# A drain on GpSimd, the count of flagged batches and the branch behind it, and a new order of loads

## The chip, the cores and the metric

The kernel runs on one core of a Trainium2 chip: TensorE (PE in the rows, with PEld for its weight loads), VectorE (DVE), ScalarE (ACT), GpSimd (POOL) and SyncE (SP), and 16 transfer engines that all queues share. A name with a q (POOLq) is an engine's sequencer, which takes instructions in order and hands them on. The metric is the time of one execution on the device in microseconds (us). In the rows the granted clock is a share of TensorE's 2.4 GHz.

## The reference

Attention with pooled keys and values, then a router that sends each row to one of eight experts. B = 8 batches, H = 8 heads, S = 576 rows, D = 64; the rows of a batch are 512 wide (all heads side by side).

```python
k_p = k.reshape(B, H, 72, 8, D).mean(axis=3)
v_p = v.reshape(B, H, 72, 8, D).mean(axis=3)
attn = softmax(q @ k_p.T / 8)
x = (attn @ v_p).transpose(0, 2, 1, 3).reshape(4608, 512)
logits = normalized(x) @ normalized(expert_emb).T / tau
expert_idx = argmax(logits)
gate_w = softmax(logits)[expert_idx]
for e in range(8):
    out[mask] = gate_w * (relu(x[mask] @ w1[e]) @ w2[e])    # 512 -> 1024 -> 512
```

## The kernel before

**One batch, one expert.** The kernel guesses one expert for each batch from the mean of its pooled values, loads the weights of that expert alone, and runs all 576 rows of the batch through it. It then looks whether a row chose another expert than the guess, or lies outside a number range. Such a batch is flagged, and a second pass behind the main part (`attend_again` and the loops around it) does it again, with every expert that is present. With these inputs no batch is flagged.

**Steps of a batch b.** Each step has a name. POOL loads K, Q and V rows, converting to 16 bits (K*b*, Q*b*.0, V*b*; for batch 0 in two parts each). DVE adds up groups of eight rows of V (VA, VB) and of K (KA, KB; in batch 0 TensorE does KA). TensorE takes the mean of the values (GM) and multiplies it with the experts' embeddings (GL); DVE finds the best (GD); PK reads that number into POOL's registers, and W1*b* and W2*b* are loads of the expert's two weight matrices, 1 MB each in 16 bits, whose addresses come from it. TensorE transposes the keys (KT, copied by KE), makes scores (SC), ACT the exponentials (EX), TensorE the weighted values (PV), DVE divides (XM), TensorE transposes (XT, copied by XE into xt). RT and RE find each row's best expert, NA to ND the gate. The FFN is H (16 steps, each 4 matmuls, relu by HE) and Y (four chunks of 128 rows, 8 matmuls each, and YL for the last 64 rows), scaled by YE, YF and YG and stored by SP (ST, SL; the second half of the very last chunk by ACT).

**The order.** `Plan.order` makes one fixed order for all engines before anything runs, in a model of times: at each point it takes the step that can start soonest, among equals the one with the lowest priority number, to which TUNED adds a value by name. The loads are an exception: they are issued in the order of LOADS. Where the model sees TensorE wait, `keep_warm` matmuls without use are put ahead of the step (L813). The weights have four buffers, K, V and Q two each, the output tiles 18. A store waits for one load of the list BEHIND. Everything inside `tc.manual_schedule()` is issued in this order; what is written behind that block is placed by the framework, which may issue an instruction sooner where nothing holds it.

**Behind the main part** stand a drain of POOL (L996), a read of the number n_i into the registers of all five engines (L997), and the second pass, a loop from 0 to that number. n_i is made by `presence`: PR, PP (a matmul, L869) and PX (eight short DVE steps, L872 to L884), whose priority puts them at the very end.

Lines of the rows: L319 loads K or V rows, L325 Q rows, L343 W1, L349 W2, L359 is PK's read, L448 the additions of VA and KA, L518 GL, L523 and L524 GD, L548 transposes q, L650 copies xt, L707 H, L719 Y, L725 YL, L733 YF, L337 stores.

Of the kernel before, what the change touches and what calls it, by code (L numbers as in the profile page):

```python
# [16 lines left out]
ALU = mybir.AluOpType  # L17
# [46 lines left out]
}  # L64
LOADS = """
V0.0 V0.1 K0.0 K0.1 Q0.0 Q0.1 V1 PK0 W10 K1 Q1.0 W20 V2 PK1 W11 K2 Q2.0 V3 W21 V4 K3 PK2 W12
Q3.0 PK3 W22 K4 W13 Q4.0 V5 Q5.0 PK4 W23 W14 K5 K6 V6 PK5 W24 W15 Q6.0 V7 Q7.0 PK6 W25 K7
W16 PK7 W26 W17 W27
# [145 lines left out]
def kernel(  # L214
# [103 lines left out]
    def load_rows(a, b, raw, g0=0, g1=G):  # L318
        return nc.gpsimd.dma_start(  # L319
            out=raw.rearrange("p h t d -> p h (t d)")[g0:g1],  # L320
            in_=a[b].rearrange("h (g t) d -> g h (t d)", g=G)[g0:g1])
# [86 lines left out]
    def attention(b, base, xt):  # L408
# [8 lines left out]
        for c, src, raw in (("V", v, vr), ("K", k, kr)):  # L417
            if b == 0:
                add(n(c, 0), 'POOL', 0.9, at_load(n(c, 0)),
                    lambda src=src, raw=raw: load_rows(src, b, raw.tile, 0, 64),  # L420
                    takes=[raw], mode=(16, 2.78 if c == "V" else 2.7, 1.2), late=0.9)
                add(n(c, 1), 'POOL', 0.6, at_load(n(c, 1)),
                    lambda src=src, raw=raw: load_rows(src, b, raw.tile, 64),
                    uses=[raw], mode=(8, 1.25 if c == "V" else 0.3, 1.2), late=0.9)
            else:
                add(n(c), 'POOL', 0.8, at_load(n(c)),
                    lambda c=c, src=src, raw=raw: note(n(c), load_rows(src, b, raw.tile)),
                    takes=[raw], mode=wire(ROWS_DMA), tail=tails.get(n(c), 0.0), late=0.9)
        if b == 0:
            for i in range(NQ):  # L430
                add(n("Q", i), 'POOL', 0.8, at_load(n("Q", i)), lambda i=i: load_q(b, qq, i, 1),
                    takes=[] if i else [qq], uses=[qq] if i else [], mode=(16, 1.3 + i, 1.2), late=0.9)
# [34 lines left out]
        if b == 0:  # L467
# [22 lines left out]
            [n("V"), "XM0.4" if b == 1 else None] if b else [n("GC")], uses=[vr], late=0.1)  # L490
# [226 lines left out]
    def y_mm(hT, w2, c, p):  # L717
        for w in range(8):
            nc.tensor.matmul(out=p, lhsT=hT[w][:, ts(c, 128)], rhs=w2[:, w // 2, w % 2, :],  # L719
                             start=(w == 0), stop=(w == 7))  # L720
# [261 lines left out]
    presence(B * PERIOD + 8.0)  # L982

    with tc.manual_schedule():
# [5 lines left out]
        for s in order:  # L990
            if s not in first:
                if s.fill:
                    keep_warm(s.fill_on, s.fill)
                s.run()

    nc.gpsimd.drain()  # L996
    n_val = nc.values_load(n_i[0:1, 0:1], min_val=0, max_val=B)  # L997
    with tc.For_i(0, n_val, 1) as i:
        f_val = nc.values_load(flag_i[0:1, ds(i, 1)], min_val=0, max_val=1)
        with tc.If(f_val > 0):  # L1000
            of = lambda t: t[ds(i, 1)].squeeze(0)
            o_b = out[ds(i * S, S)]
            xt = xt_r.tiles[0]
            attend_again(of(q), of(k), of(v), xt)
            y, o = y_r.tiles[0], y_r.tiles[1]
            nc.vector.memset(y, 0.0)
            for c in range(4):
                nc.sync.dma_start(out=chunk_rows(o_b, c), in_=y)
            put_last(o_b, y)
            w1, w2 = w1_r[0].tiles[0], w2_r[0].tiles[0]  # L1010
            with tc.For_i(0, E, 1) as e:
                p_val = nc.values_load(pick_i[0:1, ds(e, 1)], min_val=0, max_val=1)
                with tc.If(p_val > 0):
                    load_w1(e, w1)
                    load_w2(e, w2)
                    gmx = ssq_all[:, 0]
                    nc.vector.tensor_copy(out=gmx, in_=oh_x[:, :, ds(e, 1)].squeeze(2))
                    nc.vector.tensor_tensor(out=gmx, in0=gmx, in1=gate_all[:, B], op=ALU.mult)
                    hT = hT_r.tiles[0:8]
                    for w in range(8):  # L1020
                        for j in range(2):
                            p = (bank.tiles + psum.tiles)[(2 * w + j) % 4]
                            h_mm(xt, w1, w, j * HALF, (j + 1) * HALF, p)
                            h_relu(p, hT[w], j * HALF, (j + 1) * HALF, 'ACT' if j else 'DVE')
                    gl = gl_all[:, B:B + 1]
                    nc.vector.tensor_copy(out=gl, in_=gmx[64:128, 4:5])
                    for c in range(5):
                        p = (bank.tiles + psum.tiles)[c % 4]
                        if c < 4:
                            y_mm(hT, w2, c, p[:, 0:DM])  # L1030
                            scale_rows(y, p[:, 0:DM], gmx[:, c:c + 1], 'DVE')
                            dst, cols = chunk_rows(o_b, c), DM
                            nc.sync.dma_start(out=o, in_=dst)
                        else:
                            yl_mm(hT, w2, p)
                            for r in range(2):
                                rows = ts(r, 64)
                                scale_rows(y[rows, 0:DH], p[rows, ts(r, DH)],
                                           gmx[rows, 4:5] if r else gl, 'DVE')
                                nc.sync.dma_start(out=o[rows, 0:DH], in_=last_rows(o_b)[r])  # L1040
                            cols = DH
                        nc.vector.tensor_tensor(out=y[:, 0:cols], in0=y[:, 0:cols],
                                                in1=o[:, 0:cols], op=ALU.add)
                        if c < 4:
                            nc.sync.dma_start(out=dst, in_=y)
                        else:
                            put_last(o_b, y)
# [35 lines left out]
```

## Time and profile before

| | |
|---|---|
| median of 3 runs | 209.63 us (208.03 to 210.13) |
| profiled execution | 210.25 us |
| its span, first to last instruction | 208.5 us |
| PE busy | 192.2 us (92%) |
| DVE, ACT, POOL busy | 140.6, 136.6, 43.0 us |
| mean granted clock | 0.971 |
| moved by the transfer engines | 38.71 MB |

The span is shorter than the execution's own time by 1.75 us, which lie outside the instructions. Matmuls are pipelined and their ends are modelled, so a busy time counts some overlap twice. A row of a timeline gives start, duration, engine, line, operation, tiles and count, and in brackets the idle time ahead of it with what ended it.

### The profile page before, as it was taken

How to read it: one execution, taken by the hardware profiler on the slowest of the kernel's cores; microseconds unless marked ns; L12 is line 12 of the kernel's file. 1: busy time of each engine (PE TensorE's matmuls, PEld its weight loads, DVE VectorE, ACT ScalarE, POOL GpSimd, SP SyncE). 2: the span in 40 equal slices, each digit the busy share in tenths (PEclk: the TensorE clock that was granted, in tenths of full speed). 3: DMA queues.
4: the chain of work that ended last, by engine and by line, in shares of the span. 5: the costliest groups of instructions: out<-in, count | busy, mean ns of one | idle time of the engine just before them, and what ended most of it. 6: DMA issues, size and time to landing. Idle time of an engine off the chain costs nothing.

```text
span 208.5 us, 5415 instructions
## 1 busy us (share of the span) xinstructions
PE 192.2 (92%) x2080; PEld 125.2 (60%) x2081; DVE 140.6 (67%) x409; ACT 136.6 (65%) x313; POOL 43.0 (21%) x59
## 2 busy tenths in 40 slices
PE   7979989899999989999999999999999999999910
PEld 5745568447765667557765676566756676586410
DVE  2355389837896898669998897879997476242130
ACT  3004876857978779767975778469967878385410
POOL 7301603603400703006201510043000600020000
PEclk9966999999999999999999999999999999999995
DMA  4992899999999999999999999989996799950330
GB/s 56 183 183 36 137 205 212 206 207 187 207 206 176 204 211 196 209 206 210 249 208 212 177 246 242 228 173 249 239 219 232 145 218 230 267 208 3 128 104 6
DMA packets 27839, 38.71 MB, mean 186 GB/s; under 512 B 4248, under 2 KB 14488, under 8 KB 27808
## 3 DMA queue, kind: packets, MB, share of 16 engines
q0 software_dynamic: 21904, 28.85, 82.4%
q1 hardware_dynamic: 5824, 9.39, 13.3%
q8 instruction: 18, 0.29, 0.6%
q14 instruction: 13, 0.11, 0.2%
q10 hardware_dynamic: 80, 0.07, 0.1%
HBM read 61.88 MB, written 9.44 MB: 342 GB/s over the span
## 4 chain that ended last, share of the span: by engine, by line
PE 55%; DMA 24%; issue 7%; POOL 4%; DVE 4%; ACT 2%; POOLq 1%; SPq 0%; DVEq 0%; ACTq 0%
PE pb L707 20%; PE pb L719 15%; DMA kr<-in_k_dram 11%; DMA vr<-in_v_dram 10%; PE pa L589 3%; PE pa L719 3%; PE pa L707 3%; PE pa L634 3%; PE pb L378 2%; DMA out_dram<-y 2%; PE pb L725 2%; POOL vr L319 2%; PE pb L387 1%; DVE vr L448 1%; ACT y L731 1%
## 5 line engine op out<-in xcount | busy, mean ns | idle before, releaser
L707 PE MATMUL pb<-xt,w 128*128 128x288 f16 (+2 forms) x432 | 61.3, 287 | 0.9 <-DMA w<-in_moe_w_dram 0.9
L707 PEld LDWEIGHTS <-w 128*128 128x128 f16 x512 | 47.0, 98 | 16.2 <-issue 4.6
L719 PE MATMUL pb<-w,hT 128*128 128x512 f16 x224 | 52.6, 379 | 0.9 <-DMA w<-in_moe_w_dram 0.9
L597 ACT ACTIVATE at<-pa 72x576 f16<-72x576 f32 (+2 forms) x64 | 38.2, 642 | 5.2 <-PE pa L589 4.8
L719 PEld LDWEIGHTS <-hT 128*128 128x128 f16 x256 | 23.2, 97 | 26.1 <-issue 2.4
L655 ACT ACTIVATE sq<-x 128x512 f16<-128x512 f16 x40 | 25.2, 630 | 13.6 <-DVE x L370 8.7
L713 ACT ACTIVATE hT<-pb 128x288 f16<-128x288 f32 (+2 forms) x74 | 28.6, 411 | 6.9 <-PE pb L707 4.9
L731 ACT ACTIVATE y<-pb,gm_all 128x512 f32<-128x512 f32 (+1 forms) x30 | 19.0, 634 | 14.9 <-PE pb L719 11.0
L370 DVE TENSOR_TENSOR x<-pa,r_all 128x512 f16<-128x512 f32 x38 | 26.3, 691 | 2.1
L548 DVE STREAM_TRANSPOSE qT<-qq 128x576 f16<-128x576 f16 x32 | 23.2, 755 | 1.3 <-DMA qq<-in_q_dram 1.3
L398 POOL TENSOR_TENSOR ssq_all<-ssq_all,half_c 128x5 f32<-128x5 f32 x8 | 10.4, 1294 | 47.1 <-ACT sq L655 47.1
L715 DVE TENSOR_SCALAR hT<-pb 128x288 f16<-128x288 f32 (+2 forms) x34 | 14.9, 447 | 7.2 <-PE pb L707 6.9
L349 POOL DMA_DIRECT2D w<-in_moe_w_dram x8 | 5.5, 688 | 65.3 <-PE pb L725 17.0
L448 DVE TENSOR_TENSOR vr<-vr 72x2048 f16<-72x2048 f16 (+1 forms) x16 | 15.1, 942 | 5.2 <-DMA vr<-in_v_dram 5.2
L813 PE MATMUL pb<-ones_m 128*128 128x256 f16 x102 | 17.1, 314 | 1.4 <-DVE half_c L820 1.4
L589 PE MATMUL pa<-qT,kpT 32*72 32x288 f16 (+2 forms) x256 | 15.7, 295 | 0.1
L378 PEld LDWEIGHTS <-x 128*128 128x128 f16 x160 | 10.8, 97 | 6.7 <-DVE x L370 3.0
L378 PE MATMUL pb<-ident_h,x 128*128 128x128 f16 x144 | 13.5, 219 | 1.4 <-DVE x L370 1.2
L634 PEld LDWEIGHTS <-at 72*128 72x128 f16 x320 | 13.1, 98 | 1.9 <-issue 0.3
L634 PE MATMUL pa<-vpx,at 72*128 72x65 f16 x304 | 14.2, 194 | 0.0
L448 DVE TENSOR_TENSOR kr<-kr 72x2048 f16<-72x2048 f16 (+1 forms) x14 | 13.2, 944 | 1.2 <-DMA kr<-in_k_dram 1.1
L650 ACT COPY xt<-pb 128x512 f16<-128x512 f16 (+1 forms) x25 | 13.0, 536 | 0.7 <-PE pb L378 0.5
(115 smaller groups left out, 200.2 us busy)
## 6 DMA issues: line engine op xcount, KB each, us to landing
w<-in_moe_w_dram POOLq DMA_DIRECT2D x16, 1024.0 KB, 17.8
out_dram<-y SPq DMA_DIRECT2D x32, 256.0 KB, 6.1
vr<-in_v_dram POOLq DMA_DIRECT2D x7, 576.0 KB, 20.0
kr<-in_k_dram POOLq DMA_DIRECT2D x7, 576.0 KB, 18.0
qq<-in_q_dram POOLq DMA_DIRECT2D x7, 576.0 KB, 16.8
out_dram<-y SPq DMA_DIRECT2D x15, 64.0 KB, 6.3
qq<-in_q_dram POOLq DMA_DIRECT2D x2, 288.0 KB, 8.9
vr<-in_v_dram POOLq DMA_DIRECT2D x1, 512.0 KB
```

The source lines that it names most:

```text
L370: nc.vector.tensor_tensor(out=x[:, ts(i, np_)], in0=pxv[:, :, 1:129].rearrange("p a (r d) -> p a r d", d=D), in1=rv.unsqueeze(3).to_broadc ...
L378: nc.tensor.transpose(out=pt.bitcast(FP16)[:, ts(w, 128)], in_=xf[:, ts(w, 128)], identity=ident_h)
L448: nc.vector.tensor_tensor(out=t[:, :, 0:m], in0=t[:, :, 0:m], in1=t[:, :, m:2 * m], op=ALU.add)
L548: nc.vector.transpose(out=qT.tile[:, a].rearrange("p t c e -> p (t c e)")[:, cols], in_=qq.tile[:, a, cols]),
L589: nc.tensor.matmul(out=tiles[m // 2].tile[0:gs, m % 2 * 512:m % 2 * 512 + (p1 - p0) * T], lhsT=kpT.tile[ts(m, R), a, c, 0:gs], rhs=qT.tile ...
L597: nc.scalar.activation(out=t.tile[:, :, p0 * T:p1 * T].rearrange("g r (p t) -> g r p t", t=T), in_=p.tile[0:G].rearrange("g (r c) -> g r c ...
L634: nc.tensor.matmul(out=px[h // 2 // np_].tile[:, o:o + 65], lhsT=at[h // 2].tile[:, h % 2, c0:c0 + 128], rhs=vp.tile[:, h // 2, 1 + h % 2 ...
L655: nc.scalar.activation(out=sq, in_=x.tile.rearrange("p a r d -> p (a r d)"), func=AF.Square, accum_out=ssq_all[:, b, c:c + 1])
L707: nc.tensor.matmul(out=p[:, 0:c1 - c0], lhsT=w1v[:, kk, w // 2, w % 2, :], rhs=xt[:, kk, c0:c1], start=(kk == 0), stop=(kk == 3))
L713: nc.scalar.activation(out=dst, in_=src, func=AF.Relu)
L719: nc.tensor.matmul(out=p, lhsT=hT[w][:, ts(c, 128)], rhs=w2[:, w // 2, w % 2, :], start=(w == 0), stop=(w == 7))
L731: nc.scalar.activation(out=dst, in_=src, func=AF.Copy, scale=g)
```

## The change

Six parts. POOL's drain moves into the block whose order is fixed, as its last instruction. The count of flagged batches gets a lower priority number, -200 instead of +8 against the end of the last period. The second pass stands in an `If` on the count, marked as the block that falls through, with a loop over all eight batches inside; a hint for the branch is placed on TensorE's queue behind the last matmul of Y7.1. V1 is loaded in two halves of four heads, V1.0 ahead of W10 and V1.1 behind it, both behind PK0. VA0 waits for GD0 rather than GC0. LOADS and TUNED are new (LOADS is shown in full, TUNED only with its first lines), and the modelled landing of K0.1 and Q0.0 is later. The steps of the second pass are the same, indented.

```diff
 TUNED = {
-    "GM5": 79.1, "Y1.0": 28.3, "RT7": 37.3, "SC6.1.1": -29.8, "VA7": 104.9, "H3.4.0": -54.3,
...
+    "SC5.1.1": -112, "H2.5.0": -2.4, "PV7.0": -11.1, "HE2.5.0": -2.5, "H6.7.1": 24.3,
...
 LOADS = """
-V0.0 V0.1 K0.0 K0.1 Q0.0 Q0.1 V1 PK0 W10 K1 Q1.0 W20 V2 PK1 W11 K2 Q2.0 V3 W21 V4 K3 PK2 W12
-Q3.0 PK3 W22 K4 W13 Q4.0 V5 Q5.0 PK4 W23 W14 K5 K6 V6 PK5 W24 W15 Q6.0 V7 Q7.0 PK6 W25 K7
-W16 PK7 W26 W17 W27
+V0.0 V0.1 K0.0 K0.1 Q0.0 Q0.1 PK0 V1.0 W10 V1.1 K1 Q1.0 W20 V2 PK1 W11 K2 Q2.0 V3 W21 PK2 K3
+W12 Q3.0 PK3 V4 W22 K4 W13 Q4.0 V5 Q5.0 W23 PK4 W14 K5 V6 K6 PK5 W24 V7 Q6.0 W15 W25 PK6
+Q7.0 K7 W16 PK7 W26 W17 W27
 """.split()
...
-    def load_rows(a, b, raw, g0=0, g1=G):
+    def load_rows(a, b, raw, g0=0, g1=G, h0=0, h1=H):
         return nc.gpsimd.dma_start(
-            out=raw.rearrange("p h t d -> p h (t d)")[g0:g1],
-            in_=a[b].rearrange("h (g t) d -> g h (t d)", g=G)[g0:g1])
+            out=raw.rearrange("p h t d -> p h (t d)")[g0:g1, h0:h1],
+            in_=a[b].rearrange("h (g t) d -> g h (t d)", g=G)[g0:g1, h0:h1])
...
-                    uses=[raw], mode=(8, 1.25 if c == "V" else 0.3, 1.2), late=0.9)
+                    uses=[raw], mode=(8, 1.25 if c == "V" else 0.6, 1.2),
+                    late=0.9 if c == "V" else 2.3)
+            elif n(c) == "V1":
+                for i in range(2):
+                    add(n(c, i), 'POOL', 0.8, at_load(n(c, i)), lambda i=i, src=src, raw=raw:
+                        load_rows(src, b, raw.tile, 0, G, i * H // 2, (i + 1) * H // 2),
+                        takes=[] if i else [raw], uses=[raw] if i else [],
+                        mode=wire(ROWS_DMA, 0.5), late=0.9)
...
-                    takes=[] if i else [qq], uses=[qq] if i else [], mode=(16, 1.3 + i, 1.2), late=0.9)
+                    takes=[] if i else [qq], uses=[qq] if i else [], mode=(16, 1.3 + i, 1.2), late=0.9 if i else 1.5)
...
         add(n("VA"), 'DVE', 1.14, pr(-0.5), lambda: halve(vr.tile, 4),
-            [n("V"), "XM0.4" if b == 1 else None] if b else [n("GC")], uses=[vr], late=0.1)
+            ([n("V")] if b > 1 else [n("V", 0), n("V", 1), "XM0.4"]) if b else [n("GD")], uses=[vr], late=0.1)
...
-            nc.tensor.matmul(out=p, lhsT=hT[w][:, ts(c, 128)], rhs=w2[:, w // 2, w % 2, :],
-                             start=(w == 0), stop=(w == 7))
+            landing[f"Y{c}"] = nc.tensor.matmul(
+                out=p, lhsT=hT[w][:, ts(c, 128)], rhs=w2[:, w // 2, w % 2, :],
+                start=(w == 0), stop=(w == 7))
...
-    presence(B * PERIOD + 8.0)
+    presence(B * PERIOD - 200.0)
...
-    nc.gpsimd.drain()
+        nc.gpsimd.drain()
+
+    with tc.issue_after(landing["Y1"].ins):
+        tc.mark_branch_hint_location("again", engines=[ENG.PE])
     n_val = nc.values_load(n_i[0:1, 0:1], min_val=0, max_val=B)
-    with tc.For_i(0, n_val, 1) as i:
-        f_val = nc.values_load(flag_i[0:1, ds(i, 1)], min_val=0, max_val=1)
-        with tc.If(f_val > 0):
...
+    with tc.If(n_val > 0, preferred_fallthrough_block=True, label="again"):
+        with tc.For_i(0, B, 1) as i:
+            f_val = nc.values_load(flag_i[0:1, ds(i, 1)], min_val=0, max_val=1)
+            with tc.If(f_val > 0):
```

## Rows read from the trace of the kernel before

**Rows 1.** The page, chain of waits: shares of the span by engine.

```profile
PE 55%; DMA 24%; issue 7%; POOL 4%; DVE 4%; ACT 2%; POOLq 1%; SPq 0%; DVEq 0%; ACTq 0%
```

**Rows 2.** Timeline of POOL, 6 to 21 us.

```profile
6.25 0.89 POOL L319 DMA_DIRECT2D vr<-in_v_dram  x1
20.31 0.79 POOL L343 DMA_DIRECT2D w<-in_moe_w_dram  x1 [13.18 <-DVE qT L548]
```

**Rows 3.** Timeline, 9 to 12 us: VA0, GL0, and the end of GD0.

```profile
9.71 1.22 DVE L448 TENSOR_TENSOR vr<-vr 72x2048 f16<-72x2048 f16 x1
...
9.86 0.24 PE L518 MATMUL pb<-enT,mv 128*128 128x8 f16 x4
...
11.13 0.17 DVE L524 FIND_INDEX8 ix_all<-mx_all,pb 128x8 uint32<-128x8 f32 x1
```

**Rows 4.** L996 and L359 (ns; first, last start), L319 landings to 20 us.

```profile
L996 POOLq DRAIN  x1: 14163/14163/14163, 4.6 to 4.6; - x1
...
L359 POOLq TENSOR_LOAD <-ix_all x1: 483/483/483, 18.8 to 18.8; - x1
...
DMA to landing us min/median/max: 5.9/8.3/12.2
```

**Rows 5.** Transfer engines, 10 to 25 us in 40 slices: busy tenths, GB/s.

```profile
DMA  9999999999999999982000000000000962999999
GB/s 223 201 214 204 209 215 246 175 144 167 167 154 159 158 153 156 156 131 38 11 14 8 0 0 0 0 0 0 0 0 0 44 44 49 180 180 218 197 202 218
```

**Rows 6.** Timelines of ACT and PE: second copy of xt, H0, Y0.

```profile
27.02 0.56 ACT L650 COPY xt<-pb 128x512 f16<-128x512 f16 x1
...
29.38 1.05 PE L707 MATMUL pb<-xt,w 128*128 128x256 f16 x8 [0.86 <-DMA w<-in_moe_w_dram]
...
41.73 1.89 PE L719 MATMUL pb<-w,hT 128*128 128x512 f16 x8 [0.92 <-DMA w<-in_moe_w_dram]
```

**Rows 7.** keep_warm (L813), H0 to Y0: stretch, PE, PEld, clock, DMA, GB/s.

```profile
29.38:40.81 11.43, 1.81 (x12) 1.01 (x12) 1.00 1.16 209
```

**Rows 8.** The body: stretch, PE, PEld, DVE, ACT, POOL, clock, DMA, GB/s.

```profile
41.70:198.90 157.20, 155.59 (x1680) 100.10 (x1679) 114.44 (x322) 115.85 (x266) 28.12 (x33) 1.00 1.03 203
```

**Rows 9.** Timeline of all engines from 197 us.

```profile
197.80 1.06 PE L725 MATMUL pb<-w,hT 128*64 128x256 f16 x16
198.79 0.31 PE L869 MATMUL pb<-ohb,ones_m 128*128 128x328 f16 x1
...
199.91 0.55 ACTq L337 DMA_DIRECT2D out_dram<-y  x1
...
200.96 0.14 DVE L884 TENSOR_SCALAR n_i<-anyf 1x1 int32<-1x1 f32 x1
```

**Rows 10.** L998 and L1078: ns min/median/max, first and last start us.

```profile
L998 PEldq COMPARE_BRANCH  x3: 97/192/3759, 201.8 to 207.4; - x3
...
L998 PEldq COMPARE_BRANCH  x1: 3759/3759/3759, 202.3 to 202.3; - x1
...
L1078 ACTq DRAIN  x1: 8/8/8, 203.8 to 203.8; - x1
...
L1078 POOLq DRAIN  x1: 1374/1374/1374, 204.5 to 204.5; - x1
...
L1078 PEldq DRAIN  x2: 8/8/8, 207.7 to 208.0; - x2
```

**Rows 11.** Timeline of DVE (VA1, VA4); the chain's piece for K3.

```profile
28.89 1.21 DVE L448 TENSOR_TENSOR vr<-vr 72x2048 f16<-72x2048 f16 x1
...
67.90 1.22 DVE L448 TENSOR_TENSOR vr<-vr 72x2048 f16<-72x2048 f16 x1 [1.33 <-DMA vr<-in_v_dram]
...
48.72 22.67 DMA kr<-in_k_dram
```

**Rows 12.** Granted clock early on; columns as in rows 8.

```profile
10.80:11.90 1.10, 0.00 (x1) 0.01 (x1) 1.05 (x5) 0.00 (x0) 0.00 (x0) 1.00 1.13 212
12.00:18.50 6.50, 6.04 (x31) 3.86 (x30) 3.05 (x8) 0.64 (x2) 0.00 (x0) 0.50 0.75 125
```

More of the change, by code (lines that the diff above doesn't have):

```diff
@@ L994 @@
                 s.run()
-    nc.gpsimd.drain()
+        nc.gpsimd.drain()
+    with tc.issue_after(landing["Y1"].ins):
+        tc.mark_branch_hint_location("again", engines=[ENG.PE])
     n_val = nc.values_load(n_i[0:1, 0:1], min_val=0, max_val=B)
-    with tc.For_i(0, n_val, 1) as i:
-        f_val = nc.values_load(flag_i[0:1, ds(i, 1)], min_val=0, max_val=1)
-        with tc.If(f_val > 0):
[L1001 to L1047, printed above, removed]
@@ new lines @@
+    with tc.If(n_val > 0, preferred_fallthrough_block=True, label="again"):
+        with tc.For_i(0, B, 1) as i:
+            f_val = nc.values_load(flag_i[0:1, ds(i, 1)], min_val=0, max_val=1)
+            with tc.If(f_val > 0):
+                of = lambda t: t[ds(i, 1)].squeeze(0)
+                o_b = out[ds(i * S, S)]
+                xt = xt_r.tiles[0]
+                attend_again(of(q), of(k), of(v), xt)
+                y, o = y_r.tiles[0], y_r.tiles[1]
+                nc.vector.memset(y, 0.0)
+                for c in range(4):
+                    nc.sync.dma_start(out=chunk_rows(o_b, c), in_=y)
+                put_last(o_b, y)
+                w1, w2 = w1_r[0].tiles[0], w2_r[0].tiles[0]
+                with tc.For_i(0, E, 1) as e:
+                    p_val = nc.values_load(pick_i[0:1, ds(e, 1)], min_val=0, max_val=1)
+                    with tc.If(p_val > 0):
+                        load_w1(e, w1)
+                        load_w2(e, w2)
+                        gmx = ssq_all[:, 0]
+                        nc.vector.tensor_copy(out=gmx, in_=oh_x[:, :, ds(e, 1)].squeeze(2))
+                        nc.vector.tensor_tensor(out=gmx, in0=gmx, in1=gate_all[:, B], op=ALU.mult)
+                        hT = hT_r.tiles[0:8]
+                        for w in range(8):
+                            for j in range(2):
+                                p = (bank.tiles + psum.tiles)[(2 * w + j) % 4]
+                                h_mm(xt, w1, w, j * HALF, (j + 1) * HALF, p)
+                                h_relu(p, hT[w], j * HALF, (j + 1) * HALF, 'ACT' if j else 'DVE')
+                        gl = gl_all[:, B:B + 1]
+                        nc.vector.tensor_copy(out=gl, in_=gmx[64:128, 4:5])
+                        for c in range(5):
+                            p = (bank.tiles + psum.tiles)[c % 4]
+                            if c < 4:
+                                y_mm(hT, w2, c, p[:, 0:DM])
+                                scale_rows(y, p[:, 0:DM], gmx[:, c:c + 1], 'DVE')
+                                dst, cols = chunk_rows(o_b, c), DM
+                                nc.sync.dma_start(out=o, in_=dst)
+                            else:
+                                yl_mm(hT, w2, p)
+                                for r in range(2):
+                                    rows = ts(r, 64)
+                                    scale_rows(y[rows, 0:DH], p[rows, ts(r, DH)],
+                                               gmx[rows, 4:5] if r else gl, 'DVE')
+                                    nc.sync.dma_start(out=o[rows, 0:DH], in_=last_rows(o_b)[r])
+                                cols = DH
+                            nc.vector.tensor_tensor(out=y[:, 0:cols], in0=y[:, 0:cols],
+                                                    in1=o[:, 0:cols], op=ALU.add)
+                            if c < 4:
+                                nc.sync.dma_start(out=dst, in_=y)
+                            else:
+                                put_last(o_b, y)
```

53 rows, old and new, of the table TUNED are left out of this document.

## The prediction

> **What bounds the kernel now.** I read the chain of waits first: it runs 55% over TensorE and 24% over transfers [rows 1], so the question is where each of them sets the time. I then went through the span in three stages.
>
> *The start, to 41.7 us.* POOL issues the early loads, V1 last, at 6.25 us, and then nothing until W10 at 20.31 us [rows 2]. W10 needs only PK0, the read of the first chosen expert. DVE has written that index by 11.13 + 0.17 = 11.30 us [rows 3], yet the read starts at 18.8 us [rows 4]. Between the two stands a DRAIN on POOL's sequencer, from line 996, which the code has behind all steps: it starts at 4.6 us and lasts 14.163 us, to 18.77 us [rows 4]. It ends 0.3 us after V1 has landed (6.25 + 12.2 = 18.45 us [rows 4], V1 being the slowest of the row loads counted there). So the drain is issued in the midst of the first loads, and holds POOL until they have landed. The transfer engines show the price: of the 40 slices of 0.375 us from 10 us on, they are busy to about the 18th (16.9 us) and again from about the 31st (21.9 us), with hardly a byte between [rows 5]. That is a hole of 5.0 us.
>
> TensorE then waits for the load stream twice: before H0 at 29.38 us (W10), and for 0.92 us before Y0 at 41.73 us [rows 6]; Y0 starts when W20 is there. Between the two, 1.81 us are keep_warm matmuls [rows 7], which are no work.
>
> *The body, 41.7 to 198.9 us.* TensorE is busy 155.59 of 157.20 us, at a granted clock of 1.00, which is the 2.4 GHz level [rows 8]. Only 1.6 us of waiting are left: the body is a solid block of matmuls, and when Y0 starts earlier, the end follows.
>
> *The tail, 198.9 to 208.5 us.* The last matmuls of the FFN start at 197.80 us and take 1.06 us. DVE scales, and then counts the flagged batches; n_i stands at 200.96 + 0.14 = 201.10 us [rows 9]. All five engines wait for it and branch over the second pass. ACT is at its drain at 203.8 us; POOL, at 204.5 us, has a drain of 1.374 us, to 205.9 us. TensorE has one branch of 3.759 us, begun at 202.3 us, and reaches its drain only at 207.7 us [rows 10]. The end at 208.5 us hangs on that branch.
>
> **The change part by part.** The sum is made against the profiled execution: 210.25 us, a span of 208.5 us and 1.75 us around it that the change does not touch. The median of the three runs is 209.63 us, 0.62 us less, which is taken off at the end.
>
> *Drain moved behind the last step.* PK0 then waits for GD0 alone, and VA0 is moved behind GD0 as well. Before, the maximum of the guess stood behind VA0 on DVE (9.71 + 1.22 us), though the guess's matmuls were begun at 9.86 us and take 0.24 us [rows 3]. With 0.6 us for the maximum and the index, GD0 should be done near 10.7 us. From the read's start to the first issue behind it took 20.31 - 18.8 = 1.5 us. Behind PK0's wait stand V1.0, W10, V1.1, K1, Q1 and W20, so V1.0 is issued near 12.2 us. W10's transfer began 1.6 us after its issue (20.31 to 21.9 us), so V1.0 flows from 13.8 us on. V1 no longer fills the stretch before 16.9 us: 3.5 us of it were V1's (0.59 MB at the 154 to 175 GB/s of these slices [rows 5]), and the loads ahead of it end at 13.4 us. The hole shrinks from 5.0 us to 0.4 us or less. The same bytes lie ahead of W20 as before, so W20 lands about 4.8 us earlier, at 36.9 us.
>
> Can H0 keep up? It needs two copies of xt from batch 0's attention, the second done at 27.02 + 0.56 = 27.6 us [rows 6], which the hole does not touch. H0 and what is woven into it took 11.43 us, from 29.38 us to the wait before Y0, less 1.81 us of keep_warm [rows 7]: 9.6 us. So H0 is done at 37.2 us, 0.3 us behind W20: what is late next is H0 itself. Y0 moves by **4.5 us** (bounds 4.1, with a hole of 0.4 us and H0 late by as much more, and 5.0, the hole closed and the attention a little sooner). Behind the drain's new place stands only POOL's read of the count, and W27 has long landed by then: nothing.
>
> *V1 in halves.* One more issue on POOL (at most 0.89 us, the whole V1's [rows 2]) and 1.7 us of transfer ahead of W10, whose own transfer (21.9 to 29.38 us) then ends near 23 us: ahead of the 27.6 us when H0 can use it. V1 is first read at 28.89 us [rows 11] and lands near 25 us. It costs nothing; without these 4 us of cover, 1.7 us.
>
> *New order of loads.* PK2 goes ahead of K3, W12 and Q3, so these wait for GD2 instead of standing behind V4. K3 landed 22.67 us after its issue at 48.72 us [rows 11]: it waits in the stream, not at its issue, and an issue near 48 us still comes long before its turn. V4 goes behind PK3; DVE takes it the moment it lands, at 67.90 us [rows 11], in the middle of batch 2, and batch 4 is far off. Nothing.
>
> *New priorities (TUNED), later planned landings of K0.1 and Q0.0.* The trace cannot show an order that has not run. A better one can gain at most the 1.6 us of waits left in the body [rows 8]; a worse one could open as much. The planned landings put some more keep_warm matmuls ahead of KA0, where TensorE idles anyway and then runs at half clock [rows 12]. I take **-0.5 us** (bounds -1.6 and +1.6), since the earlier stream relieves some of these waits.
>
> *Count sooner.* Its matmul moves in among the Y7 matmuls: 0.31 us by its row [rows 9], less when pipelined. The hint is one instruction of TensorE's sequencer, where the short ones take 0.1 to 0.2 us [rows 10]. I take **+0.2 us** (0 to 0.5). Its DVE steps fit in beside: DVE is busy only 114 of the body's 157 us [rows 8].
>
> *Tail.* Each engine reads n_i as soon as its own work ends. TensorE: 198.86 us, plus the 1.2 us from n_i to the long branch (201.1 to 202.3), plus 0.2 us for a branch that hits, plus 1.6 us on to its drain (206.06 to 207.7): 201.9 us. ACT issues the last store at 199.91 + 0.55 = 200.46 us [rows 9] and then needs the 2.7 us that it took from n_i to its drain: 203.2 us. The final exchange took 0.8 us (207.7 to 208.5), so the end falls at 204.0 instead of 208.5 us: 4.5 us. Were POOL's drain still last, behind ACT's 0.64 us of head start, it would end at 205.3 us, the span at 206.1 us: 2.4 us. POOL has nothing left to do by then, so I stay near the first: **-4.0 us**.
>
> Sum: 210.25 - 4.5 - 0.5 + 0.2 - 4.0 = 201.45 us; less 0.62 us, **200.8 us**.
>
> By the Trainium skill (Runtime: NRT & Kernel Launch, Instruction fetch mechanics) a taken branch whose target lies outside the pages held waits for a fetch, and prefetch is purely sequential. The 3.759 us agree with the first half; by the second the hint would fetch nothing, which is the first rival. The Trainium skill (VectorE: DVE Perf Modes, The DRAIN you can't avoid) knows, besides DVE's pipe flush, only drains of about 12 ns; by it the second rival would hold. The row of 14.163 us speaks against that.
>
> **The rivals.** *The hint brings nothing.* TensorE then reaches its drain at 198.86 + 1.2 + 3.76 + 1.6 = 205.4 us and the end is 206.2 us: the tail gives 2.3 us instead of 4.0, **202.5 us**. For it: the hint stands only one Y and the YL matmuls ahead of the branch, some 3 us, less than the fetch took.
>
> *The head gives nothing,* because something other than the drain held the read, or H0 does not keep up. For it: the profile names a DVE transpose as what ended POOL's 13.18 us of idling [rows 2]. Against: neither the read nor W10 uses that tile, and the read starts where the drain ends. 210.25 - 0.5 + 0.2 - 4.0 - 0.62 = **205.3 us**.
>
> *More than forecast:* tail 4.5 us, head 5.0 us, all waits of the body gone: 0.5 + 0.5 + 1.1 us more, **198.7 us**.
>
> *Slower: TensorE's clock.* Behind 1.1 us with no matmul (10.8 to 11.9 us), the granted clock was 0.50, the 1.2 GHz level, from 12 to 18.5 us [rows 12]. A load stream that comes at other times than planned may leave gaps where no keep_warm stands. Each us at half clock costs 0.5 us of matmuls. To end 1% slower than before (2.1 us), it must also eat the 8.8 us gained: 22 us at half clock, over three such stretches. That is the point from which it decides, and it gives **212 us**. Against: the clock stayed at 1.00 through both waits after 29 us [rows 7, 8].
>
> *The change does not do what it says:* the drain is still issued early and the branch still misses, about **209 us**.
>
> **How the numbers follow.** Forecast 0.60, hint without effect 0.15, no head gain 0.07, more 0.12, clock 0.04, not done 0.02. The forecast's terms reach from 198.5 us, all at their best, to 205.2 us, all at their worst; the hint's rival lies inside. Leaving the last 0.8 us of the worst corner and adding 0.5 us of the runs' scatter below, 198.0 to 204.4 us holds forecast, hint and more, 0.87, less their corners. A measurement here tells 1% (the three runs lie between 208.03 and 210.13 us). Faster by over 1%: 0.60 + 0.15 + 0.07 + 0.12 = 0.94; within: 0.02; slower: 0.04.
>
> **What would show it.** No long DRAIN on POOL before 20 us; the first issue behind PK0 near 12 us; no hole in the transfers from 17 to 22 us; Y0 at about 37 us; YL7 ending near 194 us; n_i written before it; no TensorE branch of several us; the last drain within 5.5 us of YL7's end. The prediction is wrong if Y0 moves by less than 4 us, if the body grows past 159 us, or if another engine's exit takes the place of TensorE's branch.

## The result and the profile after

The changed kernel takes 201.03 us (median of 4 runs, 200.87 to 201.43) against 209.8 us (4 runs): the ratio is 0.9606, with a 95% interval of 0.9557 to 0.9656. The forecast was 200.8 us, in a range of 198.0 to 204.4 us. The profiled execution took 201.43 us, its span is 199.8 us.

The chain of waits of the changed kernel, by engine (as [rows 1]):

```profile
PE 75%; DMA 11%; DVE 5%; issue 2%; ACT 2%; POOL 1%; SPq 0%; POOLq 0%; ACTq 0%; DVEq 0%
```

Transfers fell from 24% to 11% of the chain. The start first: POOL's drain and PK0's read, by line (as [rows 4]), then POOL's timeline (as [rows 2]) and the transfer engines from 10 to 25 us in slices of 0.375 us (as [rows 5]), all of the changed kernel:

```profile
L1004 POOLq DRAIN  x1: 2935/2935/2935, 180.4 to 180.4; - x1
...
L360 POOLq TENSOR_LOAD <-ix_all x1: 486/486/486, 11.3 to 11.3; - x1
```

```profile
12.66 0.76 POOL L320 DMA_DIRECT2D vr<-in_v_dram  x1 [6.42 <-DVE mx_all L536]
13.41 0.78 POOL L344 DMA_DIRECT2D w<-in_moe_w_dram  x1
```

```profile
DMA  9999999400091479999999999999999999999999
GB/s 206 221 197 203 221 221 190 93 6 0 0 80 8 38 120 167 172 147 202 180 180 186 137 169 186 191 229 208 191 208 218 197 186 192 194 199 208 199 201 183
```

The drain now stands at 180.4 us, where no load is behind it. PK0's read comes at 11.3 us instead of 18.8 us, and W10 is issued at 13.41 us instead of 20.31 us. The hole in the transfers has shrunk from 5.0 us to 2.0 us (about 13 to 15 us), not to 0.4 us.

H0 and Y0 on TensorE's timeline (as [rows 6]), then the body (as [rows 8]) and the granted clock of 12 to 18.5 us (as [rows 12]):

```profile
24.19 1.47 PE L715 MATMUL pb<-xt,w 128*128 128x256 f16 x12
...
29.23 0.25 PE L513 MATMUL pa<-mean_c,vpx 72*128 72x1 f16 x4 [0.45 <-DVE vpx L470]
...
35.02 0.71 PE L822 MATMUL pb<-ones_m 128*128 128x256 f16 x5
...
36.19 1.37 PE L822 MATMUL pb<-ones_m 128*128 128x256 f16 x11
...
37.89 0.39 PE L822 MATMUL pb<-ones_m 128*128 128x256 f16 x2
38.12 1.89 PE L727 MATMUL pb<-w,hT 128*128 128x512 f16 x8
```

```profile
38.12:193.73 155.61, 154.97 (x1682) 100.30 (x1679) 116.98 (x337) 115.10 (x266) 28.70 (x33) 1.00 1.03 205
...
12.00:18.50 6.50, 5.76 (x58) 3.80 (x57) 4.71 (x11) 2.40 (x5) 5.43 (x7) 1.00 0.79 117
```

No row of H0 or Y0 shows a wait for a transfer any more. Ahead of Y0 stand 18 keep_warm matmuls (L822), planned before anything ran; W20, issued at 16.47 us, landed 21.3 us later, at 37.8 us, 0.3 us before Y0. Inside H0 TensorE waits 0.45 us for the added-up rows of V1 (L513). That comes from V1's second half, issued at 14.19 us and landed 12.4 us later, at 26.6 us; DVE waited for it before VA1 (list of waits, 20 to 39 us):

```profile
DVE vr L456 <- DMA vr<-in_v_dram: 0.8, 1, 0.8
```

Y0 is 3.6 us sooner (41.73 to 38.12 us), and the body is 1.5 us shorter (157.1 to 155.6 us).

The tail: timeline (as [rows 9]), and by line the branch over the second pass and the exits (as [rows 10]):

```profile
189.87 0.14 DVE L893 TENSOR_SCALAR n_i<-anyf 1x1 int32<-1x1 f32 x1
...
192.67 1.06 PE L734 MATMUL pb<-w,hT 128*64 128x256 f16 x16
...
194.79 0.55 ACTq L338 DMA_DIRECT2D out_dram<-y  x1
```

```profile
L1090 PEldq BRANCH_PREFETCH_HINT  x1: 50/50/50, 187.1 to 187.1; - x1
...
L1009 PEldq COMPARE_BRANCH  x1: 487/487/487, 193.4 to 193.4; - x1
...
L1090 PEldq DRAIN  x1: 8/8/8, 194.3 to 194.3; - x1
...
L1009 SPq EVENT_SEMAPHORE  x7: 17/17/17, 197.6 to 198.1; - x7
...
L1090 SPq DRAIN  x3: 7/7/7, 199.0 to 199.3; - x3
```

TensorE's branch takes 0.49 us instead of 3.759 us, and TensorE is at its drain 0.6 us behind the end of YL7 (193.73 us). But now SP ends last: it stands still until 197.6 us, 2.3 us behind the end of the last store's issue (194.79 + 0.55 us), and reaches its drain at 199.0 us. That it waits for the landing of that store is read from these times; no run tests it. From the end of YL7 to the end of the span it takes 6.1 us, before 9.6 us: 3.6 us gained. Head 3.6, body 1.5 and tail 3.6 us make 8.7 us, which is the difference of the spans.

### The profile page after: what moved, and what is told of

It is laid out like the page before. It is cut to its first block, busy times and chain, and to the rows that moved or that the text cites. A ratio compares the mean times of both kernels' runs of the same rounds, so it can differ in the third digit from the quotient of the medians.

```text
span 199.8 us, 5384 instructions
## 1 busy us (share of the span) xinstructions
PE 189.7 (95%) x2085; PEld 125.1 (63%) x2086; DVE 140.9 (71%) x411; ACT 134.6 (67%) x311; POOL 45.2 (23%) x60
## 4 chain that ended last, share of the span: by engine, by line
PE 75%; DMA 11%; DVE 5%; issue 2%; ACT 2%; POOL 1%; SPq 0%; POOLq 0%; ACTq 0%; DVEq 0%
PE pb L715 23%; PE pb L727 23%; DMA kr<-in_k_dram 8%; PE pa L597 5%; PE pa L715 5%; PE pb L822 5%; PE pa L642 3%; PE pb L379 3%; DMA out_dram<-y 3%; PE pb L734 2%; PE pa L727 2%; PE pb L388 2%; DVE qT L556 1%; DVE x L371 1%; DVE kr L456 1%
## 5 line engine op out<-in xcount | busy, mean ns | idle before, releaser
L715 PE MATMUL pb<-xt,w 128*128 128x288 f16 (+2 forms) x408 | 59.1, 287 | 0.1
L727 PE MATMUL pb<-w,hT 128*128 128x512 f16 x232 | 54.4, 379 | 0.0
L740 ACT ACTIVATE y<-pb,gm_all 128x512 f32<-128x512 f32 (+1 forms) x32 | 20.4, 636 | 13.9 <-PE pb L727 9.7
L399 POOL TENSOR_TENSOR ssq_all<-ssq_all,half_c 128x5 f32<-128x5 f32 x8 | 11.9, 1484 | 46.2 <-ACT sq L663 46.2
L822 PE MATMUL pb<-ones_m 128*128 128x256 f16 x108 | 17.2, 307 | 1.4 <-DVE half_c L829 1.4
L370 DVE RECIPROCAL r_all<-pa 128x8 f32<-128x8 f32 x38 | 7.5, 198 | 13.8 <-PE pa L642 13.3
L715 PE MATMUL pa<-xt,w 128*128 128x288 f16 (+2 forms) x104 | 16.7, 286 | 0.0
L642 PEld LDWEIGHTS <-at 72*128 72x128 f16 x320 | 13.9, 98 | 3.4 <-issue 1.3
L642 PE MATMUL pa<-vpx,at 72*128 72x65 f16 x304 | 14.8, 194 | 0.5 <-ACT at L605 0.5
L723 DVE TENSOR_SCALAR hT<-pb 128x288 f16<-128x288 f32 (+1 forms) x27 | 11.9, 446 | 2.8 <-PE pb L715 2.4
L822 PEld LDWEIGHTS <-ones_m 128*128 128x128 f16 x108 | 10.6, 108 | 5.0 <-issue 1.7
```

Source lines behind the costliest of these rows:

```text
L642: nc.tensor.matmul(out=px[h // 2 // np_].tile[:, o:o + 65], lhsT=at[h // 2].tile[:, h % 2, c0:c0 + 128], rhs=vp.tile[:, h // 2, 1 + h % 2 ...
L715: nc.tensor.matmul(out=p[:, 0:c1 - c0], lhsT=w1v[:, kk, w // 2, w % 2, :], rhs=xt[:, kk, c0:c1], start=(kk == 0), stop=(kk == 3))
L727: landing[f"Y{c}"] = nc.tensor.matmul(out=p, lhsT=hT[w][:, ts(c, 128)], rhs=w2[:, w // 2, w % 2, :], start=(w == 0), stop=(w == 7))
L740: nc.scalar.activation(out=dst, in_=src, func=AF.Copy, scale=g)
L822: nc.tensor.matmul(out=p[:, 256:512], lhsT=ones_m[:, 0:128], rhs=ones_m[:, 0:256], start=True, stop=True)
```

## Experiments

**The drain alone, and the tail alone.** Two kernels from the one before, and a third with both:

```diff
@@ drain alone
-    nc.gpsimd.drain()
+        nc.gpsimd.drain()        # last in the ordered block
@@ tail alone
-    presence(B * PERIOD + 8.0)
+    presence(B * PERIOD - 200.0)
+    with tc.issue_after(landing["Y1"].ins):
+        tc.mark_branch_hint_location("again", engines=[ENG.PE])
-    with tc.For_i(0, n_val, 1) as i:
+    with tc.If(n_val > 0, preferred_fallthrough_block=True, label="again"):
+        with tc.For_i(0, B, 1) as i:
```

> The kernel before with one edit: the drain is the last instruction of the ordered block. Loads, priorities, count and branch are as before. Theory (the drain held POOL until V1 had landed, and W20's landing sets Y0): no drain of several us before 20 us; W10 is issued near 12.9 us instead of 20.3 us (index written at 11.3 us, 1.5 us from the read's start to the issue); no hole in the transfers from 17 to 22 us; Y0 near 37.3 us instead of 41.73 us; the tail as before, 9.6 us from the last YL matmul to the end of the span. Ratio to before 0.979 (4.4 us less). Rival (the new order and the sooner attention of batch 0 brought the head forward, not the drain): ratio above 0.995.

> The kernel before with the tail's parts alone: count sooner, the second pass in an If, the hint on TensorE's queue. The drain stays early, loads and priorities are as before. Theory: Y0 stays at 41.7 us, the tail shrinks from 9.6 us to the 6.1 us of the changed kernel, which are set by the landing of the last store; ratio 0.983 (3.5 us less). Rival (the tail is worth the whole missed branch of 3.76 us and the 2.2 us of counting on DVE): ratio 0.972.

> The kernel before with both: the drain last in the ordered block, and the tail's parts. Loads, V1 in one piece, priorities and planned landings as before. Theory: the two gains add, 4.4 + 3.5 us, ratio 0.962; the new order of loads, the halves of V1 and the new priorities are then worth nothing beyond 1 us against the 0.9606 of the changed kernel. Rival (the shorter body of the changed kernel, 155.6 us against 157.1 us, comes from the new priorities): ratio 0.968 or more, with a body of 157 us.

Against 208.73 us of the kernel before: the drain alone 204.03 us (ratio 0.979, interval 0.971 to 0.987), the tail alone 205.77 us (0.9867, 0.9803 to 0.9932), both 200.56 us (0.9598, 0.9541 to 0.9654). So 4.7 us and 3.0 us, and 8.2 us together. The transfers (10 to 25 us) and Y0 of the kernel with the drain moved alone:

```profile
DMA  9999999999999899999999999999999999999999
```

```profile
36.13 1.89 PE L719 MATMUL pb<-w,hT 128*128 128x512 f16 x8
```

No hole at all, since V1, issued at 6.24 us, flows while PK0 waits; Y0 is 5.6 us sooner than in the profile of before (3.4 us sooner than in that of the tail alone, which has the early drain too and Y0 at 39.57 us), and 2 us sooner than in the changed kernel. Its tail is still 9.6 us (YL ends at 192.56 us, the span at 202.2 us). In the tail's kernel YL ends at 196.87 us and the span at 203.0 us: 6.1 us, as in the changed kernel. The drain and the tail carry the whole gain. The rival that the order did it is refuted: with the old order the two reach the time of the changed kernel.

Is the body's 1.5 us the new order's? The profiles answer in part. From Y0 to the end of YL7 the old order took 157.1 us (before), 157.3 us (tail alone), 156.4 us (drain alone) and 156.5 us (both); the new one 155.4 to 155.6 us in the changed kernel and in eight of the nine others that have it (below), 156.7 us in the ninth (two tiles). So some 0.9 us belong to the new order: with the drain alone and with both, TensorE waits 0.9 to 1.0 us for DVE in this stretch (ahead of the XT of a batch and of a GL), in the changed kernel 0.3 us. The rest, some 0.6 us, may go with the sooner stream. Ahead of Y0 the changed kernel is 1.6 us behind the kernel with both (38.12 against 36.49 us), so it loses more there than the new order brings.

**The drain back in the changed kernel.**

```diff
-        nc.gpsimd.drain()
+    nc.gpsimd.drain()            # behind the ordered block, as before
```

> The changed kernel with one edit: the drain stands behind the ordered block again, where the framework places it. Theory: it is issued early, between Q0.1 and PK0, and holds POOL until Q0.1 has landed (no longer V1, which now stands behind PK0), to about 13.5 us instead of 11.27 us; the stream behind it, W20 and Y0 come 2 to 2.5 us later, ratio 0.971. Rival (a drain costs about nothing, the order of loads was the matter): ratio 0.961, as the changed kernel. Second rival (it costs all that it cost before): ratio 0.979 or more.

206.11 us (0.9869, 0.9810 to 0.9929), 5.1 us slower than the changed kernel: the drain was the matter, and it cost twice what I expected. The second rival came true, that it costs all that it cost before. By line, and on TensorE's timeline; then two stretches (PE, PEld, DVE, ACT, POOL, granted clock, DMA, GB/s):

```profile
L1005 POOLq DRAIN  x1: 10843/10843/10843, 4.1 to 4.1; - x1
```

```profile
27.43 2.74 PE L715 MATMUL pb<-xt,w 128*128 128x256 f16 x12 [3.65 <-DMA w<-in_moe_w_dram]
...
42.70 1.89 PE L727 MATMUL pb<-w,hT 128*128 128x512 f16 x8
```

```profile
23.00:27.00 4.00, 0.77 (x16) 0.53 (x12) 2.02 (x6) 2.09 (x7) 0.00 (x0) 0.85 1.14 201
27.00:33.00 6.00, 5.57 (x28) 4.03 (x29) 2.23 (x3) 1.88 (x6) 1.25 (x1) 0.53 1.24 202
```

The drain ended at 14.9 us, not at 13.5 us: most bytes of the loads ahead of it had moved by 13 us, but single packets of POOL's queue went on to 14.2 us. Then TensorE had no matmul for 3.65 us before H0, and the clock fell: 0.53 of 2.4 GHz in the mean of the next 6 us, mostly its 1.2 GHz level. Twelve matmuls took 2.74 us that take 1.47 us in the changed kernel. H0 started 3.2 us later than in the changed kernel and took 1.5 us longer up to its last matmuls; Y0 is 4.6 us late, and the body is 155.6 us again.

**Hint and count.** The changed kernel without the hint, with the late count, and with neither:

```diff
@@ no hint
-    with tc.issue_after(landing["Y1"].ins):
-        tc.mark_branch_hint_location("again", engines=[ENG.PE])
@@ late count
-    presence(B * PERIOD - 200.0)
+    presence(B * PERIOD + 8.0)
```

> The changed kernel without the hint on TensorE's queue. Theory: TensorE's branch over the second pass takes 3.76 us again instead of 0.49 us, so TensorE reaches its drain near 197.6 us instead of 194.3 us; SP, which waits for the landing of the last store, is there only at 199.0 us, so the time does not change: ratio to before as the changed kernel's, within 0.3%. Rival (the hint carries the tail's gain): 3.3 us slower than the changed kernel.

> The changed kernel with the count back at the end, behind all other steps. Theory: n_i stands 2.2 us behind the end of YL7, near 195.9 us instead of 190.0 us; TensorE then still reaches its drain near 197.5 us thanks to the hint, ACT 0.5 us later than before, SP still waits for the last store; at most 0.4 us slower. Rival (the 2.2 us of counting were on the path and come back in full): 2.2 us slower.

> The changed kernel with neither: no hint and the count at the end. Theory: the two hide the same thing from either side, and only without both does TensorE end last: n_i at 195.9 us, 1.2 us to the branch, 3.76 us for it, 0.3 us to the drain, near 201.2 us, the end near 202.0 us, 2.2 us slower than the changed kernel. Rival (they add): the sum of what the two kernels without one of them lose.

201.24 us without the hint (0.9621, 0.9574 to 0.9668), 201.02 us with the late count (0.9605, 0.9559 to 0.9651), 202.65 us with neither (0.9689, 0.9644 to 0.9734). TensorE's branch without the hint, and with neither:

```profile
L1007 PEldq COMPARE_BRANCH  x1: 4285/4285/4285, 192.7 to 192.7; - x1
```

```profile
L1007 PEldq COMPARE_BRANCH  x1: 3678/3678/3678, 195.9 to 195.9; - x1
...
L1088 PEldq DRAIN  x2: 8/8/8, 200.0 to 200.6; - x2
```

The hint works: TensorE's branch takes 0.39 to 0.49 us with it, 3.68 to 4.29 us without. Yet each of the two parts alone is enough, since then TensorE is through before SP is. From the end of YL7 to the end of the span: 6.1 us with both, 6.6 us without the hint, 5.9 us with the late count, 8.1 us with neither. So the losses do not add (0.2 and 0 us alone, 1.6 us together, where 2.2 us was expected). With neither, the tail still lies 1.6 us under the 9.6 us of before. What is left of the tail's change there is the `If` in place of the loop, and the rows fit it: the branch comes 0.6 us behind n_i instead of 1.2 us, and the drain 0.4 us behind the branch instead of 1.6 us. The `If` was not tried by itself.

**V1 ahead of PK0.** The changed kernel, with the halves of V1 moved in POOL's queue alone:

```diff
         order = plan.order(loads)
+        early = [s for s in order if s.name in ("V1.0", "V1.1")]
+        order = [s for s in order if s not in early]
+        at_pk = [s.name for s in order].index("PK0")
+        order[at_pk:at_pk] = early
```

> The changed kernel with both halves of V1 issued ahead of PK0's read, as V1 was before; nothing else is moved. Theory: V1 fills the 2 us hole that the changed kernel still has in its transfers from 13 to 15 us, W20 lands 1.5 to 2 us earlier, Y0 comes near 36.4 us instead of 38.1 us and the end follows, 1 to 1.7 us faster than the changed kernel. Rival (the body has taken up the later start, as its 155.6 us against 156.5 us hint): no change.

200.25 us (0.9586, 0.9539 to 0.9633), 0.8 us faster than the changed kernel and 0.8 to 1.0 us faster than those without the hint and with the late count, which were timed together with it; 1 to 1.7 us was expected. Its transfers (10 to 25 us), Y0 and body:

```profile
DMA  9999999999999999999999999999999999999999
```

```profile
36.68 1.89 PE L727 MATMUL pb<-w,hT 128*128 128x512 f16 x8
```

```profile
36.68:192.26 155.58, 154.94 (x1682) 100.25 (x1679) 116.83 (x337) 115.10 (x266) 28.72 (x33) 1.00 1.01 204
```

The hole is closed, Y0 is 1.4 us sooner, and the body stays at 155.6 us: the end follows Y0. Of the 1.4 us, 0.35 us come from an earlier H0 and 0.9 us from a shorter one, in which neither DVE nor TensorE waits for V1. W20 landed at 35.7 us (14.41 + 21.3 us), 1.0 us before Y0, so it is H0 with the keep_warm matmuls behind it that sets Y0 here. This version has the lowest median, but its interval overlaps that of the changed kernel (0.9557 to 0.9656): what carries the reading is Y0. The halves of V1 behind PK0 cost more of Y0 than the 0.9 us that the new order brings in the body.

**The guess sooner.** The changed kernel with six keep_warm matmuls fewer ahead of GM0:

```diff
-                    s.fill = max(0, int((at - was - slack) / 0.11))
+                    s.fill = max(0, int((at - was - slack) / 0.11) - (6 if s.name == 'GM0' else 0))
```

> The changed kernel with six keep_warm matmuls fewer ahead of GM0, the first step of the guess. Theory (PK0's read, and the hole of 2 us behind it, hang on GM0, which waits for these matmuls): GM0 starts 0.5 us sooner, PK0 reads at 10.7 us instead of 11.27 us, the hole shrinks by as much, Y0 and the end come 0.5 us sooner, 200.5 us. Rival (GM0 waits for the last rows of V0, not for the matmuls): no change.

GM0 starts at 8.19 us, the first issue behind PK0 at 11.81 us, Y0 at 37.18 us. For the first two that is 0.84 us sooner than in the profile of the changed kernel, but the same head without this edit has GM0 at 8.37 to 8.60 us and the issue at 11.99 to 12.21 us in three other profiles, so the edit is worth some 0.2 us: GM0 now waits for V0's rows (0.40 us), as the rival had it. The time is 201.25 us (0.9638, 0.9605 to 0.9671), not 200.5 us. Y0 lies between 37.4 and 38.1 us in the four profiles with the unchanged head, so what this brings is within their scatter. A miss: the timing does not show it.

**The planned landings, and TensorE's clock.** The changed kernel with the old planned landings of K0.1 and Q0.0 (fewer keep_warm matmuls ahead of KA0); then the kernel with V1 first, with none there:

```diff
@@ old landings
-                    uses=[raw], mode=(8, 1.25 if c == "V" else 0.6, 1.2),
-                    late=0.9 if c == "V" else 2.3)
+                    uses=[raw], mode=(8, 1.25 if c == "V" else 0.3, 1.2), late=0.9)
@@ none ahead of KA0
-                    s.fill = max(0, int((at - was - slack) / 0.11))
+                    s.fill = 0 if s.name == 'KA0.0' else max(0, int((at - was - slack) / 0.11))
```

> The changed kernel with the planned landings of K0.1 and Q0.0 as they were before, so with fewer keep_warm matmuls ahead of KA0. Theory (these matmuls only insure against TensorE's clock falling to half while it waits for K0): most runs as the changed kernel, 201.0 us, some up to 2 us slower, at a lower mean clock. Rival (they are a steady part of the gain): all runs 1 us or more slower.

> The kernel with V1 issued ahead of PK0's read, without the 13 keep_warm matmuls ahead of KA0, so that TensorE has no matmul for some 1.4 us before K0 lands. Theory (the clock falls to the 1.2 GHz level there, as in the profile of before): KA0 takes 3.6 us instead of 1.9 us, batch 0's attention and H0 come 2 to 3 us later, and Y0 is then set by H0 near 37.7 us instead of by W20 near 36.7 us; 0.5 to 1.5 us slower than with them. Rival (W20's landing covers it): no change.

201.2 us (0.9633, 0.9599 to 0.9667; six runs from 200.67 to 201.63) with the old landings: no steady gain, and none of the six runs was slow as the theory allowed. Without any, 202.54 us (0.9708, 0.9669 to 0.9747), 2.3 us slower than the kernel that it was made from. TensorE's timeline and the clock of that kernel:

```profile
11.16 3.48 PE L480 MATMUL pb<-kr,ident_h 72*128 72x256 f16 x16 [1.09 <-DMA kr<-in_k_dram]
```

```profile
12.00:18.50 6.50, 6.04 (x38) 3.62 (x37) 3.58 (x9) 0.64 (x2) 3.96 (x5) 0.53 1.17 194
```

Behind 1.1 us without a matmul the clock falls, KA0 takes 3.48 us instead of 1.9 us, H0 starts at 26.00 us instead of 23.84 us, and Y0 comes at 38.84 us instead of 36.68 us. It is more than the 0.5 to 1.5 us expected: W20 landed at 34.6 us (14.42 + 20.2 us), so with the hole closed H0 behind batch 0's attention, with the keep_warm matmuls planned behind it, sets Y0.

In the profile of before the clock fell in the same way [rows 12], but its Y0 waited for W20 [rows 6], so that profile does not show what the fall cost. Among the runs of the kernel before that were timed with the experiments, the six with a mean clock of 0.965 to 0.967 have a median of 210.0 us, the fifteen with 0.978 or more 208.6 us; that fits a cost of some 1.5 us, but it is no experiment. The tail alone, with the same start, kept its clock. Its drain, and two waits of TensorE:

```profile
L997 POOLq DRAIN  x1: 12842/12842/12842, 4.6 to 4.6; - x1
```

```profile
27.98 1.05 PE L707 MATMUL pb<-xt,w 128*128 128x256 f16 x8 [2.52 <-DMA w<-in_moe_w_dram]
...
39.57 1.89 PE L719 MATMUL pb<-w,hT 128*128 128x512 f16 x8 [0.17 <-DMA w<-in_moe_w_dram]
```

W20 was issued at 21.30 us there instead of 22.65 us, since the drain ended 1.3 us sooner, and Y0 came at 39.57 us instead of 41.73 us. Behind the 2.52 us without a matmul ahead of H0 the granted clock was 1.00 from 28 to 34 us, so the length of a gap alone does not tell whether the clock falls.

**Two tiles for the last rows.** YG7 (ACT) starts only behind YF7 (DVE), though both need only YL7. From the version with V1 first:

```diff
+        y2 = Buf(y_r) if b == B - 1 else y
...
-            scale_rows(y.tile[rows, 0:DH], p.tile[rows, ts(r, DH)],
+            scale_rows((y2 if r else y).tile[rows, 0:DH], p.tile[rows, ts(r, DH)],
```

> The kernel with V1 issued ahead of PK0's read, and the very last 64 rows scaled into two tiles instead of one, so that ACT's YG7 need not wait for DVE's YF7. Theory (the end hangs on the landing of the last store, which ACT issues behind YG7): YG7 starts 0.5 us sooner, the store is issued and lands as much sooner, the tail shrinks from 6.3 to 5.8 us, 199.75 us against 200.25 us. Rival (SP's exit is set by something else than that store): no change.

200.28 us (0.9587, 0.9554 to 0.9619): no change. ACT's row shows that the wait is still there:

```profile
194.20 0.47 ACT L740 ACTIVATE y<-pb,gm_all 64x256 f32<-64x256 f32 x1 [0.82 <-DVE y L742]
```

So the shared output tile was not what made it wait, and whether a sooner store shortens the tail was not tested. Both also read the same PSUM tile; whether that holds ACT was not tried. (The profile is of the slowest run, 202.11 us, with a wait of 0.9 us for DVE in the body.)

## Why the prediction was right, and where its terms were not

The time, 200.8 us against 201.03 us, and the main mechanism were right: the drain held POOL, the end follows Y0, the missed branch set the end. But the head gave 0.9 us less than forecast, the body 1.2 us more and the tail 0.4 us less; that their sum came out within 0.2 us is luck. Two of the three signs that the prediction named for being wrong did come: Y0 moved by less than 4 us between the two profiles, and another engine's exit, SP's, took the place of TensorE's branch.

*Head, 4.5 us forecast, 3.6 us between the two profiles.* The step that failed is "the hole shrinks to 0.4 us or less": 2.0 us were left here, and 1.2 to 1.4 us in three other profiles with the same head (no hint, late count, neither). The loads ahead ended near 13 us rather than 13.4 us. V1.0 was issued at 12.66 us rather than 12.2 us, since GD0 was done at 11.2 us rather than 10.7 us (GM0 stood behind keep_warm matmuls); in the three others this part came as forecast, with GD0 at 10.6 to 10.8 us and the issue at 11.99 to 12.21 us. V1.0's first bytes came 1.4 us behind its issue, but the transfers were full again only near 15 us. The other size that failed is V1 behind PK0, which was costed at nothing, with 4 us of cover for its reader. The cover was not there: V1 landed at 26.6 us, not near 25 us, and with batch 0's attention earlier its reader was due sooner; VA1 waited 0.8 us and TensorE 0.45 us inside H0. The run with V1 first puts the place of V1 at 0.8 us of time and 1.4 us of Y0.

I took the profile of before as it stood, and so the half clock from 12 to 18.5 us as part of the early stage, with room behind W20. The run without keep_warm matmuls shows that such a stretch costs 2.3 us when W20 is early. In the kernel with the drain back there is a second place, H0 behind a late W10: so the early drain cost more than its hole there, since the gap that it left before H0 was followed by half clock (H0 1.5 us longer). The rival on the clock had expected this of the changed kernel; it came in two of the experiments and in the profile of before, and the changed kernel kept 1.00 from 10.8 to 193.7 us.

*H0's start.* "Batch 0's attention, which the hole does not touch" did not hold: H0 began at 24.19 us, 3.4 us ahead of my 27.6 us, since the attention ran at the full clock (KA0 1.91 us instead of 3.57 us). So H0 was not what was late next; its last matmuls began at 34.47 us, and W20 landed 0.9 us later than forecast, at 37.8 us. Y0 followed the keep_warm matmuls planned for that wait.

*Body, -0.5 and +0.2 us forecast, -1.5 us measured,* inside the bound of -1.6 us. I gave it to the earlier stream; some 0.9 us of it are the new order's, which has 155.6 us wherever Y0 starts (36.68, 38.12, 42.70 us).

*Tail, 4.0 us forecast, 3.6 us measured.* I let the end hang on ACT's and TensorE's exits. TensorE was far sooner (0.6 us behind YL7 instead of 3.0 us, since its sequencer read n_i before the last matmul had ended, and since I had kept the 1.2 us and 1.6 us around the branch of before), ACT too (3.1 instead of 4.3 us); what I had not priced was SP's exit, by its times the landing of the last store. It would have been there before too, hidden by TensorE's branch. The rival "the hint brings nothing" came true in the timing, but not for its reason: the hint saves 3.3 to 3.8 us of TensorE's time, yet with the count sooner SP's exit hides it. Its argument was wrong as well: the hint was issued at 187.1 us, 6.3 us ahead of the branch and not some 3 us, with three chunks of Y and YL behind it.

The moves in the order of loads that I costed at nothing (PK2 ahead of K3, V4 behind PK3), and VA0 behind GD0, were not tried by themselves; the old order and the whole new one end within 0.5 us of each other.

## What to carry to other kernels

Look in the trace for what an engine's sequencer is holding, not only for what the engine does: one drain without an order of its own, placed by the framework among the first loads, cost 4.7 us here, and the idle time was put down to another instruction. When a wait is moved ahead of a load, ask what the transfer engines do meanwhile, and whether the load's reader moves forward as well: here the independent loads were better off ahead of the read that waits. At the end of a kernel several exits run side by side, so removing the longest gives only the distance to the next; two remedies for the same exit do not add.

## What the runs showed of the hardware that was not expected

An early drain on POOL, with loads of its own queue under way, lasted 14.16 us (before), 12.84 us (tail alone) and 10.84 us (drain back). By the trace's records of the transfers the last packet of POOL's queue ended at 18.16, 16.77 and 14.21 us, and the drain 0.62, 0.66 and 0.71 us behind it: it follows the transfers, not the program. At the end of the changed kernel, with the last such packet 5.6 us past, it still took 2.9 us, to 1.7 us behind POOL's last instruction. A taken branch on TensorE across the second pass costs 3.7 to 4.3 us, with the hint 0.4 to 0.5 us. TensorE's clock fell to the 1.2 GHz level behind 1.1 us without matmuls before KA0 (before, and without keep_warm matmuls) and in the 3.65 us before H0 (drain back), and stayed there for 6 to 7 us each time; behind 2.52 us without matmuls before H0 (tail alone) it stayed at 2.4 GHz.
